# Zero fill of the key and value gradients through a float32 view of the bfloat16 outputs

## The chip, the cores and the metric

The kernel runs on one core of one Trainium2 chip. The metric is the device time of one execution in microseconds; before the change its median is 797.53 us over two runs (797.41 to 797.66). One further execution was taken by the hardware profiler, and all rows below come from that one.

## What is computed

The reference is a decode step with a sliding-window attention and a squared-ReLU layer, and all its gradients. Cut to what matters here:

```python
def _A_ref(x, k_cache, v_cache, wq, wo):        # caches: (2, 8, 32768, 128) bf16
    W = min(4096, max(256, Sk // 4))            # 4096
    k = jnp.repeat(k_cache[:, :, Sk - W:, :], rep, axis=1)
    v = jnp.repeat(v_cache[:, :, Sk - W:, :], rep, axis=1)
    ...
    p = _softmax(scores, axis=-1)
    o = jnp.einsum("bhqk,bhkd->bhqd", p, v)
    return ... @ wo
...
xn = _layernorm(x)
out = x + _A_ref(xn, ...) * _silu(_B_ref(xn, ...))
_out, _vjp = jax.vjp(_f, A_x, A_k_cache, A_v_cache, A_wq, A_wo, B_w1, B_b1, B_w2, B_b2)
```

Only the last 4096 of 32768 cache rows enter the computation. The gradients of both caches have the caches' full shape, so 28672 rows of each of the 2 x 16 (batch, head) regions are zero and have to be written: 2 x 16 x 28672 x 128 elements of two bytes, 234.9 MB. The other outputs together are small beside this.

## The kernel before

**The zero fill.** A tile zt of 128 partitions x 7168 bytes (type uint8, lines 80 and 81) is cleared once by VectorE. The function zf (lines 91 to 103) issues one DMA on GpSimd's queue that writes zeros over a run of rows of one region. Its source is zt, one byte for each element; its destination is the bfloat16 output, so that the DMA casts each zero byte to a two-byte zero as it writes. A partition's share is cut into groups of zg = 56 rows (32 rows in every fourth region, line 117), and the source is repeated over the groups with to_broadcast. One contiguous run of the destination is thus 56 x 128 x 2 = 14336 bytes, or 8192 bytes with 32 rows.

A region's main job (line 134) fills with 128 partitions as far as that goes and then the remainder. Six regions have a job ahead of it (line 127, by the skip plan of line 116) with 120 partitions. The counter zcur (line 102) follows the partition counts of all fills, and zf_tiny (lines 108 to 114) puts in fills of some elements to bring the counter to a wanted value; the plan decides by it where the 120-partition jobs fall. zf_tiny has a slice of its own and doesn't go through zf.

**The order of the work.** Nine fill jobs are issued ahead of everything else (line 159). The others are handed out over the 16 blocks of the main loop (line 448) and what is left after it (line 571). On GpSimd they stand in one instruction stream with the multiplications that make bdq and bddo (line 443).

**The rest.** After a short prologue (layer norm, the squared-ReLU layer forward, transposes of w1 and w2), the main loop runs over 8 heads and 2 batches. For each it loads 1 MB of the v and of the k window on SyncE's queue (lines 368 and 370), one block ahead; transposes them on TensorE; makes scores, softmax and their gradients; and makes dv and dk by matmuls against bddo and bdq, which GpSimd prepares. dv_st and dk_st (1 MB each, bfloat16) are stored from ScalarE's queue (lines 535 and 542), as are the gradients of wo and wq (lines 357 and 569), and the weight slices are loaded on that queue too. An epilogue makes the gradients of w1, w2, the biases and x, and stores them from SyncE's queue (lines 592 to 672). The last of the dw1 stores is on line 649.

Of the kernel before, what the change touches and what calls it, by code (L numbers as in the profile page):

```python
# [12 lines left out]
F32 = mybir.dt.float32  # L13
# [4 lines left out]
def kernel(  # L18
# [27 lines left out]
    _, HKV, SK, DH = A_k_cache.shape  # L46
# [33 lines left out]
    zt = const.tile([P, ZE], mybir.dt.uint8, name="zt")  # L80
# [4 lines left out]
    def _kof(n):  # L85
        for k in range(16, 0, -1):
            if n % k == 0:
                return k
        return 1

    def zf(o, q, r0, nent, rows_per_ent, zg=None):
        zg = zg or ZG
        b, hk = divmod(q, HKV)
        nr = nent * rows_per_ent
        if rows_per_ent % zg == 0:
            v = o[b, hk, r0:r0 + nr, :].rearrange("(r p g) d -> p r (g d)", p=nent, g=zg)
            src = zt[0:nent, 0:zg * DH].unsqueeze(1).to_broadcast([nent, rows_per_ent // zg, zg * DH])
        else:
            v = o[b, hk, r0:r0 + nr, :].rearrange("(p g) d -> p (g d)", p=nent)
            src = zt[0:nent, 0:rows_per_ent * DH]  # L100
        dma_zero.dma_start(out=v, in_=src)  # L101
        zcur[0] = (zcur[0] + _kof(nent)) % 16
        return r0 + nr
# [16 lines left out]
    def region_jobs(qi):  # L120
        o = out_2 if qi < B * HKV else out_3
        q = qi % (B * HKV)
        st = {"r": 0}

        zg = ZG_OF(qi)

        def j_skip():
            eng, nch = skip_plan[qi]
            adv = (eng + 1 - zcur[0]) % 16
            if adv:  # L130
                zf_tiny(adv)
            st["r"] = zf(o, q, st["r"], 120, nch * ZG)

        def j_main():
            rem = ZR - st["r"] - (P if qi == SCRAP_Q else 0)
            n_full = rem // (P * zg)
            if n_full:
                st["r"] = zf(o, q, st["r"], P, n_full * zg, zg)
            rem = ZR - st["r"] - (P if qi == SCRAP_Q else 0)
            if rem:  # L140
                nent = [n for n in (128, 64, 32, 16) if rem % n == 0][0]
                st["r"] = zf(o, q, st["r"], nent, rem // nent)
            if qi == SCRAP_Q:
                st["r"] = zf(o, q, st["r"], P - 1, 1)
                if scrap_pos[0] < DH:
                    zf_tiny(DH - scrap_pos[0])

        return ([j_skip] if qi in skip_plan else []) + [j_main]
# [554 lines left out]
```

## Time and profile before

| what | value |
|---|---|
| median of two runs | 797.53 us |
| span of the profiled execution | 795.6 us |
| busy PE / DVE / ACT / POOL | 402.2 / 265.6 / 210.0 / 315.3 us |
| bytes moved by DMA | 326.85 MB, mean 411 GB/s |
| zero fill: DMAs on line 101 | 42, mean issue 769 ns |
| last store issued (line 649) | 730.3 us |

The span runs from the first to the last instruction of the profiled execution. The median of the runs is 1.9 us above it. The page has the busy time of the engines, the span in 40 slices of 19.9 us, the DMA queues (q0 is GpSimd's, q1 SyncE's, q10 ScalarE's), a chain of waits, the costliest groups of instructions, and the DMA issues with their time to landing. A packet is one descriptor's worth of data, here one contiguous run; its size in the records is that of its destination. Shares of 16 engines can add to a little over 100%, since the records of packets overlap at their ends.

### The profile page before, as it was taken

The numbers are of one execution on the slowest core, as the hardware profiler recorded it, in microseconds if no ns is written. First come the engines' busy times: TensorE is split into PE (matmuls) and PEld (weight loads), VectorE is DVE, ScalarE is ACT, GpSimd is POOL, SyncE is SP. The second block draws the span as 40 slices with busy tenths as digits, with TensorE's granted clock in tenths as the row PEclk, the third lists the DMA queues.
The fourth block names the chain that finished last, engine by engine and source line by source line (L and its number), as shares of the span: only waits on it lengthen the run. The fifth ranks groups of instructions, "written<-read, shape, count | busy, mean of one in ns | idle before, by whom it ended". The sixth has DMA issues, their size and how long they took to land.

```text
span 795.6 us, 11174 instructions
## 1 busy us (share of the span) xinstructions
PE 402.2 (51%) x4776; PEld 277.0 (35%) x4776; DVE 265.6 (33%) x550; ACT 210.0 (26%) x384; POOL 315.3 (40%) x249
## 2 busy tenths in 40 slices
PE   4566444573446546634475358446733686276000
PEld 3466124352424444423272326243522353131000
DVE  3243322361323423611352136223611453754000
ACT  2232310360133314501342135203600450034000
POOL 3001791098109531881080719800826192700000
PEclk9978655895588659955697589656955795555555
DMA  9999999999999999999999999999999999999981
GB/s 361 421 422 424 427 427 423 431 416 417 423 428 424 417 420 428 421 421 421 428 420 422 424 426 423 425 422 430 422 420 422 430 425 420 431 429 425 416 340 57
DMA packets 37794, 326.85 MB, mean 411 GB/s; under 512 B 3008, under 2 KB 3144, under 8 KB 11016
## 3 DMA queue, kind: packets, MB, share of 16 engines
q0 software_dynamic: 20288, 234.89, 71.6%
q10 hardware_dynamic: 11296, 50.34, 16.5%
q1 hardware_dynamic: 6160, 40.91, 13.2%
q8 instruction: 37, 0.61, 0.3%
q14 instruction: 13, 0.11, 0.0%
HBM read 45.62 MB, written 280.50 MB: 410 GB/s over the span
## 4 chain that ended last, share of the span: by engine, by line
DMA 48%; PE 19%; DVE 9%; issue 6%; ACT 5%; POOL 2%; another core or an unknown queue 2%; ACTq 0%; POOLq 0%; DVEq 0%
DMA out_dram<-dv_st 20%; DMA knat<-in_A_k_cache_dram 15%; DMA out_dram<-dwo_st 7%; DMA out_dram<-zt 5%; ACT dv_st L193 3%; DMA out_dram<-dk_st 2%; PE ov L531 2%; PE s_ps L467 2%; PE ok L538 2%; PE tp L463 2%; PE dp_ps L506 2%; PE tp L495 1%; PE dq_ps L524 1%; DVE dk_st L195 1%
## 5 line engine op out<-in xcount | busy, mean ns | idle before, releaser
L443 POOL TENSOR_TENSOR bddo<-dorep,maskbd 128x1024 bf16<-128x1024 bf16 x64 | 133.6, 2114 | 90.5 <-ACT dorep L438 90.5
L443 POOL TENSOR_TENSOR bdq<-qrep,maskbd 128x1024 bf16<-128x1024 bf16 x64 | 133.4, 2110 | 0.0
L101 POOL DMA_DIRECT2D out_dram<-zt x42 | 32.2, 769 | 203.5 <-DMA out_dram<-zt 201.8
L463 PE MATMUL tp<-ident_bf,knat 128*128 128x128 bf16 x512 | 56.6, 280 | 74.8 <-DMA knat<-in_A_k_cache_dram 71.3
L463 PEld LDWEIGHTS <-knat 128*128 128x128 bf16 x512 | 44.7, 127 | 98.8 <-DMA knat<-in_A_k_cache_dram 72.8
L193 ACT CAST dv_st<-ov 128x512 bf16<-128x512 f32 x80 | 44.4, 593 | 125.3 <-PE ov L531 81.2
L531 PE MATMUL ov<-bddo,p_blk 128*128 128x512 bf16 x128 | 51.4, 486 | 50.3 <-ACT dv_st L193 39.6
L195 DVE CAST dv_st<-ov 128x512 bf16<-128x512 f32 x48 | 33.2, 693 | 100.7 <-PE ov L531 57.9
L355 PE MATMUL wps<-ds_rows,o_rows_alt 2*128 2x512 bf16 x32 | 17.4, 600 | 73.0 <-ACT dwo_st L193 73.0
L538 PE MATMUL ok<-bdq,ds_blk 128*128 128x512 bf16 x128 | 46.2, 422 | 15.9 <-DVE dk_st L195 6.0
L195 DVE COPY kT<-tp 128x1024 bf16<-128x1024 bf16 x48 | 32.8, 682 | 58.4 <-PE tp L463 58.4
L193 ACT CAST dk_st<-ok 128x512 bf16<-128x512 f32 x80 | 44.6, 589 | 26.7 <-PE ok L538 22.5
L495 PE MATMUL tp<-ident_bf,vnat 128*128 128x128 bf16 x512 | 42.9, 235 | 7.6 <-DVE vT L195 4.5
L495 PEld LDWEIGHTS <-vnat 128*128 128x128 bf16 x512 | 36.6, 107 | 26.3 <-issue 24.4
L195 DVE CAST dk_st<-ok 128x512 bf16<-128x512 f32 x48 | 32.8, 689 | 28.1 <-PE ok L538 24.8
L195 DVE CAST dwo_st<-wps 128x512 bf16<-128x512 f32 x16 | 11.1, 691 | 85.5 <-DMA out_dram<-dv_st 81.8
L193 ACT CAST dwo_st<-wps 128x512 bf16<-128x512 f32 x16 | 8.7, 588 | 112.0 <-DMA out_dram<-dv_st 111.6
L195 DVE COPY vT<-tp 128x1024 bf16<-128x1024 bf16 x48 | 32.3, 682 | 14.7 <-PE tp L495 14.5
L531 PEld LDWEIGHTS <-p_blk 128*128 128x128 bf16 x128 | 12.7, 119 | 59.6 <-ACT dv_st L193 25.5
L538 PEld LDWEIGHTS <-ds_blk 128*128 128x128 bf16 x128 | 10.3, 103 | 40.2 <-DVE dv_st L195 17.3
L519 PEld LDWEIGHTS <-ds_blk 128*128 128x128 bf16 x16 | 1.7, 104 | 64.2 <-issue 64.2
L195 DVE COPY woT_s<-tp 128x1024 bf16<-128x1024 bf16 x8 | 19.5, 2432 | 10.5 <-PE tp L394 10.5
(240 smaller groups left out, 674.9 us busy)
## 6 DMA issues: line engine op xcount, KB each, us to landing
out_dram<-zt POOLq DMA_DIRECT2D x25, 7168.0 KB, 135.2
out_dram<-zt POOLq DMA_DIRECT2D x4, 6720.0 KB, 146.6
vnat<-in_A_v_cache_dram SPq DMA_DIRECT2D x16, 1024.0 KB, 16.6
knat<-in_A_k_cache_dram SPq DMA_DIRECT2D x16, 1024.0 KB, 20.9
out_dram<-dv_st ACTq DMA_DIRECT2D x16, 1024.0 KB, 22.0
out_dram<-dk_st ACTq DMA_DIRECT2D x16, 1024.0 KB, 17.1
out_dram<-zt POOLq DMA_DIRECT2D x1, 6144.0 KB, 100.5
out_dram<-zt POOLq DMA_DIRECT2D x1, 5120.0 KB, 98.6
```

The source lines that it names most:

```text
L101: dma_zero.dma_start(out=v, in_=src)
L193: nc.scalar.copy(out=out_ap, in_=in_ap)
L195: nc.vector.tensor_copy(out=out_ap, in_=in_ap)
L355: nc.tensor.matmul(wps[:], lhsT=o_rows_alt[:, j, :], rhs=ds_rows[:, :], start=True, stop=True)
L443: nc.gpsimd.tensor_tensor(out=bd[:, c0:c0 + BDC, :], in0=rep[:, :].unsqueeze(1).to_broadcast([P, BDC, DH]), in1=maskbd[:, c0:c0 + BDC, :], ...
L463: nc.tensor.transpose(tp[:, j, :], knat[:, g * 8 + j, :], ident_bf[:, :])
L467: nc.tensor.matmul(s_ps[:], lhsT=zq[:, 31 - c:159 - c], rhs=kT[:, c, :], start=(c == 0), stop=(c == NC_ - 1))
L495: nc.tensor.transpose(tp[:, j, :], vnat[:, g * 8 + j, :], ident_bf[:, :])
L506: nc.tensor.matmul(dp_ps[:], lhsT=zdo[:, 31 - c:159 - c], rhs=vT[:, c, :], start=(c == 0), stop=(c == NC_ - 1))
L524: nc.tensor.matmul(dq_ps[:], lhsT=knat[:, c, :], rhs=dsT[:, c, :], start=(c == 0), stop=(c == NC_ - 1))
L531: nc.tensor.matmul(ov[:], lhsT=p_blk[:, :], rhs=bddo[:, g * 4:(g + 1) * 4, :].rearrange("p c d -> p (c d)"), start=True, stop=True)
L538: nc.tensor.matmul(ok[:], lhsT=ds_blk[:, :], rhs=bdq[:, g * 4:(g + 1) * 4, :].rearrange("p c d -> p (c d)"), start=True, stop=True)
```

## The change

The fill's destination is viewed as float32 in place of bfloat16, so that it has half as many elements of twice the size, and the source slice is halved to match. Each zero byte of the source becomes four zero bytes of the output. The runs of the destination, the number of DMAs, their order and the tile zt are unchanged; half of zt is no longer read. zf_tiny keeps its two-byte destination.

```diff
@@ -93,11 +93,11 @@
         b, hk = divmod(q, HKV)
         nr = nent * rows_per_ent
         if rows_per_ent % zg == 0:
-            v = o[b, hk, r0:r0 + nr, :].rearrange("(r p g) d -> p r (g d)", p=nent, g=zg)
-            src = zt[0:nent, 0:zg * DH].unsqueeze(1).to_broadcast([nent, rows_per_ent // zg, zg * DH])
+            v = o[b, hk, r0:r0 + nr, :].bitcast(F32).rearrange("(r p g) d -> p r (g d)", p=nent, g=zg)
+            src = zt[0:nent, 0:zg * DH // 2].unsqueeze(1).to_broadcast([nent, rows_per_ent // zg, zg * DH // 2])
         else:
-            v = o[b, hk, r0:r0 + nr, :].rearrange("(p g) d -> p (g d)", p=nent)
-            src = zt[0:nent, 0:rows_per_ent * DH]
+            v = o[b, hk, r0:r0 + nr, :].bitcast(F32).rearrange("(p g) d -> p (g d)", p=nent)
+            src = zt[0:nent, 0:rows_per_ent * DH // 2]
         dma_zero.dma_start(out=v, in_=src)
         zcur[0] = (zcur[0] + _kof(nent)) % 16
         return r0 + nr
```

## The prediction

> **What bounds the kernel now.** I read the page's time slices first, since they say whether one resource is full all the time.
>
> ```profile
> DMA  9999999999999999999999999999999999999981
> GB/s 361 421 422 424 427 427 423 431 416 417 423 428 424 417 420 428 421 421 421 428 420 422 424 426 423 425 422 430 422 420 422 430 425 420 431 429 425 416 340 57
> DMA packets 37794, 326.85 MB, mean 411 GB/s; under 512 B 3008, under 2 KB 3144, under 8 KB 11016
> ```
>
> Each digit is a fortieth of the span (19.9 us). The 16 DMA engines are at 9 from the first slice to the 38th and move 416 to 431 GB/s in slices 2 to 38. No compute engine comes near this: the page's first part has PE at 402.2 us of 795.6, the others at 40% or less. So the bound is the DMA engines' throughput on 326.85 MB, and 326.85 MB over the mean of 411 GB/s is 795 us, the span itself.
>
> Next, whose bytes these are: the page's table of DMA queues.
>
> ```profile
> q0 software_dynamic: 20288, 234.89, 71.6%
> q10 hardware_dynamic: 11296, 50.34, 16.5%
> q1 hardware_dynamic: 6160, 40.91, 13.2%
> HBM read 45.62 MB, written 280.50 MB: 410 GB/s over the span
> ```
>
> Columns are packets, MB, and the time of the packets as a share of 16 engines' span. q0 is GpSimd's queue, on which the zero fill alone is issued: 32 regions x 28672 rows x 256 B = 234.88 MB. So the page counts the bytes of the destination, not of the source, which is half as large. One engine on q0 moves 234.89 MB / (0.716 x 16 x 795.6 us = 9114 us) = 25.8 GB/s; on q10, 50.34 / 2100 = 24.0; on q1, 40.91 / 1681 = 24.3. The cast queue is not the slow one.
>
> Third, the end of the span, by the windows view (columns: PE, PEld, DVE, ACT, POOL busy us, PE clock, DMA share, GB/s).
>
> ```profile
> 720.00:740.00 20.00, 9.36 (x23) 2.59 (x21) 7.02 (x12) 6.84 (x12) 0.00 (x0) 0.50 1.03 423
> 740.00:760.00 20.00, 0.00 (x0) 0.00 (x0) 0.00 (x0) 0.00 (x0) 0.00 (x0) 0.50 1.03 410
> 760.00:780.00 20.00, 0.00 (x0) 0.00 (x0) 0.00 (x0) 0.00 (x0) 0.00 (x0) 0.50 0.73 291
> 780.00:795.60 15.60, 0.00 (x0) 0.00 (x0) 0.00 (x0) 0.00 (x0) 0.00 (x0) 0.50 0.08 31
> ```
>
> After 740 us no engine computes: the last store, of dw1, is issued at 730.3 us (the view of line 649) and the last 55 us are DMA backlog alone. The engines do not run dry together: share 0.73, then 0.08, about one engine of 16 at the end. Evenly shared, the span would end 0.27 x 20.0 + 0.92 x 15.6 = 19.8 us earlier. The page's chain of waits ends at 730 us and names dv_st and knat transfers; their length is queueing behind this backlog, so I don't read it as a latency bound.
>
> Fourth, the zero fill's own line, in the waits view and in the page's DMA issues.
>
> ```profile
> POOL out_dram L101 <- DMA out_dram<-zt: 201.8, 16, 31.2
> POOL out_dram L112 <- DMA out_dram<-zt: 44.5, 4, 16.6
> out_dram<-zt POOLq DMA_DIRECT2D x25, 7168.0 KB, 135.2
> ```
>
> GpSimd stands 246 us waiting for earlier fills before it can issue the next. The fill is always ahead of its drain, so issue cost (42 x 769 ns = 32 us on line 101) is covered.
>
> **The price of a packet.** The trace keeps each DMA packet's duration and size. Grouped (mean ns; size is that of the destination):
>
> ```
> zero fill 1->2 byte   14336 B x13288  551    8192 B x4992  325
> w1/w2 load, no cast   14336 B x256    559
> k/v load, no cast                            8192 B x4096  326
> dv/dk store, no cast                         8192 B x4096  323
> ```
>
> From the fill's two sizes: (551 - 325) ns / (14336 - 8192) B gives 27.2 GB/s for an engine plus about 24 ns fixed. The pair that decides is the store of dv/dk against the fill at 8192 B: same direction, same destination size, and the store reads 8192 B from SBUF where the fill reads 4096. Doubling the source changes 325 to 323 ns. The time of a packet follows the destination's bytes.
>
> **What the Trainium skill says.** "DMA: Bandwidth & Descriptors", section "Where 436 GB/s comes from", gives 16 ports x 32 B x 850 MHz = 435.2 GB/s, which is 27.2 GB/s an engine: the slope above is that figure, and the slices' 416 to 431 GB/s are 96 to 99% of it. The same section names about 358 GB/s as the HBM limit of a core; the trace's 410 over the whole span contradicts that for one core alone, and the measurement decides. "SWDGE vs HWDGE vs iDMA" says that a cast needs the GpSimd path; both versions have one. "Queues, rings and completion order" says that an engine takes turns between queues at packets; the landing times of loads (knat 20.9 us for 1 MB) agree with sharing. No page that I found prices a cast by its element widths.
>
> **The change part by part.** Each region's fill describes the same HBM bytes as half as many float32 elements; a full row of the fill is 56 x 128 / 2 = 3584 elements from 3584 B of zt, where it was 7168 from 7168.
>
> Destination: 234.88 MB before and after, in the same runs of 14336 or 8192 B, so 13288 + 4992 large descriptors as before. At 551 and 325 ns: change 0.
>
> Source: read traffic from SBUF falls from 117.4 to 58.7 MB. Value taken: 0. The work that hides it is the write side of the same packet: at 27.2 GB/s the read of a large packet is 264 ns now and 132 after, beside a write of 527. If read and write ran one after the other the packet would take at least 791 ns, and it takes 551, so serial reads are excluded. Gain bound: the uncast copy of 14336 B takes 8 ns more with 7168 B more read (other direction, so only a hint); 3584 B less might then save 4 ns: 13288 x 4 / 16 engines = 3.3 us. The 8192 B pair points to -1 ns saved, that is none. If even the cover went, there is nothing to pay, since the read only shrinks.
>
> Cast to four bytes: not seen in the trace. Per destination byte it makes half as many elements, 6.8 per ns and engine at full rate, where 13.6 are sustained now; so the element rate cannot bind if it is one rate for all types. Value taken 0; lower end 0 (the destination's slope is already the ceiling); upper end open, priced as a rival.
>
> Issue: 42 instructions on line 101 and 7 on line 112, the same partition counts, so the cursor of line 102 and the skips of line 132 keep their values. Value 0; covered by 246 us of waiting on GpSimd in any case. Small leftovers (512 of 3584 B at 155 ns, 127 of 256 B at 38 ns and some more) are about 150 us of engine time, 9 us of the span, and keep their destination sizes. The memset of zt (1.55 us) is untouched. No wait is added; zf_tiny on line 112 is not edited.
>
> Sum: 795.6 + 0 = 795.6 us of span; the median of the runs lies 1.9 us above it (797.53), so 797.5 us.
>
> **The rivals.** First, a gain in the fixed part: the lighter read lets an engine start the next packet earlier. All 24 ns gone from 18280 large packets is 18280 x 24 / 16 = 27 us, giving 770; half of it gives 784. It is over 2% (16 us) from 59% of the fixed part on. For it: engines run at 423 GB/s, not 435. Against: halving the source from store to fill already bought nothing.
>
> Second, on the other side: the conversion to a four-byte output runs below the port's rate. Its place is the 13288 + 4992 large packets, its price the excess per packet. 16 us of span are 16 x 16000 / 18280 = 14 ns a packet, 2.5%: from there on the change is slower by 2%. If the output came at half rate, 14336 B would take 527 ns more and 8192 B 301: (13288 x 527 + 4992 x 301) / 16 = 532 us, giving 1330. For it: nothing in the trace covers this cast. Against: the two-byte cast costs nothing measurable beside a copy.
>
> Third, turn-taking: with shorter reads the fill may run further ahead inside an engine and loads land later. Nothing is lost while the queues are full, since a delayed load only lets more fill through; it costs only if the last store moves from 730 towards 770 us, or if the uneven tail of 19.8 us grows. Worth -3 to +6 us: 794 to 804.
>
> Fourth, that the narrower source is not what reaches the engines, for instance that the rows are cut otherwise: with equal descriptors it is again 797.5; twice as many would cost 18280 x 24 ns / 16 = 27 us, giving 825. Nothing in the trace speaks for it.
>
> **How the numbers follow.** No change, 794 to 800: 0.75. A small gain down to 782: 0.07. A gain of over 2%: 0.05. A small loss up to 813, by the tail or turn-taking: 0.06. A loss of over 2%, slow cast or split rows: 0.07. About 2% is what a measurement here can tell from no change. Faster 0.05, same 0.75 + 0.07 + 0.06 = 0.88, slower 0.07. The range of 788 to 803 takes the likeliest case, the nearer half of each small one, and leaves out under 0.2.
>
> **What would show it.** Right: q0 at about 20288 packets, 234.89 MB and 71 to 72%; slices at 416 to 431 GB/s; packets of 14336 B at 551 ns; GpSimd's waits for zt near 246 us. Wrong: a q0 share over 73% with longer packets (slow cast); a packet count that doubles (split rows); packets under 540 ns or slices near 435 GB/s (a gain in the fixed part); unchanged packets with a longer last slice (the tail).

## The result, and the profile after

The changed kernel takes 807.58 us (807.22 to 807.93), the kernel before 797.53: ratio 1.0126, 95% interval 1.0096 to 1.0155. It is slower by 1.3%, where no change was forecast. A further measurement gave 807.89 us, ratio 1.0130 (1.0112 to 1.0148).

The profiled execution has a span of 805.4 us, 9.8 longer than before. First its time slices, which answer to the lines shown of before.

```profile
DMA  9999999999999999999999999999986999989996
GB/s 367 420 422 427 430 423 427 429 421 416 423 429 432 415 423 421 427 430 422 423 421 429 413 375 424 423 431 414 429 330 247 364 391 421 431 351 427 421 396 268
DMA packets 37794, 326.85 MB, mean 406 GB/s; under 512 B 3008, under 2 KB 3144, under 8 KB 11016
```

Packets and bytes are the same to the last digit, and so is the rate in most slices. What is new is a hole: slices 30 to 33 (584 to 664 us) move 247 to 391 GB/s; slices 24 and 36 are down too, at 375 and 351. In return the end, where the kernel before fell from 340 to 57, is fuller at 396 and 268.

Next the DMA queues.

```profile
q0 software_dynamic: 20288, 234.89, 72.6%
q10 hardware_dynamic: 11296, 50.34, 22.7%
q1 hardware_dynamic: 6160, 40.91, 17.8%
```

The fill (q0) barely moved, from 71.6 to 72.6%. The copies did: ScalarE's queue went from 16.5 to 22.7% and SyncE's from 13.2 to 17.8% with unchanged packets. The packet records say where: each copy ends in up to 16 packets of 4 bytes, read here as those that announce its completion. They last 808 ns in the mean, against 43 before (1568 of them on the two queues), while a copy's data packets of 8192 B went from 325 to 342 ns only.

The waits view (us in total, times, longest us) has another order. Two lines of the kernel before:

```profile
POOL bddo L443 <- ACT dorep L438: 90.5, 10, 20.0
PE tp L463 <- DMA knat<-in_A_k_cache_dram: 71.3, 9, 16.1
```

And of the kernel after:

```profile
POOL bddo L443 <- ACT dorep L438: 240.0, 14, 35.0
PE tp L463 <- DMA knat<-in_A_k_cache_dram: 115.2, 12, 19.7
POOL out_dram L101 <- DMA out_dram<-zt: 61.0, 3, 31.9
```

Before, GpSimd waited 201.8 us on line 101 for fills ahead of it: the fill always had work waiting. Now it waits 61.0 there and 240.0, instead of 90.5, for the blocks' own work (dorep), ahead of which it cannot issue more fill. PE waits 115.2 us for k, where it waited 71.3. The stores of dk show how far the blocks have fallen back, in the view of line 542; the first of these lines is of the kernel before.

```profile
L542 ACTq DMA_DIRECT2D out_dram<-dk_st x16: 338/338/354, 106.3 to 713.1; - x16
```

The second is of the kernel after.

```profile
L542 ACTq DMA_DIRECT2D out_dram<-dk_st x16: 338/338/358, 105.9 to 783.6; - x16
```

The first block ends as early as before, the sixteenth 70.5 us later. The way there is uneven: by the starts of the 16 dk stores the lateness is 19.8 us at the fourth block, 47.7 at the seventh and 82.1 at the eleventh, and then it shrinks a little. The last dw1 store is issued at 800.3 us instead of 730.3, and the span ends 5.1 us after it.

```profile
L649 SPq DMA_DIRECT2D out_dram<-dw_st_7325 x1: 332/332/332, 800.3 to 800.3; - x1
```

So the end is now set by the blocks and the epilogue, no more by a backlog of fill.

The bytes give a balance, by the windows view. It says when the rate was lower and when higher, not yet why. The kernel before:

```profile
560.00:720.00 160.00, 89.32 (x1047) 56.66 (x1047) 69.98 (x131) 43.68 (x83) 72.88 (x53) 0.65 1.05 425
720.00:795.60 75.60, 9.36 (x23) 2.59 (x21) 7.02 (x12) 6.84 (x12) 0.00 (x0) 0.50 0.76 304
```

The kernel after:

```profile
560.00:720.00 160.00, 88.86 (x1055) 60.55 (x1055) 51.82 (x113) 43.16 (x86) 75.01 (x58) 0.67 1.03 376
720.00:805.40 85.40, 48.29 (x426) 24.21 (x423) 37.62 (x70) 23.84 (x44) 22.41 (x17) 0.60 1.07 370
```

At the steady 424 GB/s, the hole costs 160 x (1 - 376 / 424) = 18.1 us, and 360 x 3 / 424 = 2.5 us are lost from 200 to 560 us (421 GB/s). The end gives back 75.6 x (1 - 304 / 424) = 21.4 less 85.4 x (1 - 370 / 424) = 10.9, that is 10.5 us. Together +10.1 us, for a span longer by 9.8.

### The profile page after: what moved, and what is told of

It reads as the page before. It is cut to its first block, busy times and chain, and to the rows that moved or that the text cites. A ratio compares the mean times of both kernels' runs of the same rounds, so it can differ in the third digit from the quotient of the medians.

```text
span 805.4 us, 11174 instructions
## 1 busy us (share of the span) xinstructions
PE 416.9 (52%) x4776; PEld 286.9 (36%) x4776; DVE 258.8 (32%) x550; ACT 210.2 (26%) x384; POOL 314.9 (39%) x249
## 3 DMA queue, kind: packets, MB, share of 16 engines
q0 software_dynamic: 20288, 234.89, 72.6%
q10 hardware_dynamic: 11296, 50.34, 22.7%
q1 hardware_dynamic: 6160, 40.91, 17.8%
## 4 chain that ended last, share of the span: by engine, by line
DMA 63%; PE 17%; DVE 6%; issue 5%; ACT 4%; POOL 2%; another core or an unknown queue 2%; ACTq 0%; POOLq 0%; DVEq 0%
DMA knat<-in_A_k_cache_dram 20%; DMA out_dram<-dv_st 18%; DMA out_dram<-dk_st 13%; DMA out_dram<-dwo_st 8%; DMA out_dram<-zt 5%; PE ov L531 2%; PE ok L538 2%; PE tp L463 2%; PE s_ps L467 2%; ACT dv_st L193 2%; PE dq_ps L524 1%; PE dp_ps L506 1%; PE tp L495 1%; POOL bddo L443 1%
## 5 line engine op out<-in xcount | busy, mean ns | idle before, releaser
L463 PE MATMUL tp<-ident_bf,knat 128*128 128x128 bf16 x512 | 56.6, 279 | 118.3 <-DMA knat<-in_A_k_cache_dram 115.2
L538 PE MATMUL ok<-bdq,ds_blk 128*128 128x512 bf16 x128 | 51.1, 465 | 36.2 <-ACT dk_st L193 26.7
L193 ACT CAST dk_st<-ok 128x512 bf16<-128x512 f32 x80 | 44.5, 589 | 57.4 <-PE ok L538 28.6
L495 PEld LDWEIGHTS <-vnat 128*128 128x128 bf16 x512 | 39.4, 113 | 32.9 <-issue 31.3
L495 PE MATMUL tp<-ident_bf,vnat 128*128 128x128 bf16 x512 | 45.3, 245 | 6.6 <-DVE vT L195 3.4
```

Of the source, the lines that this page charges most:

```text
L193: nc.scalar.copy(out=out_ap, in_=in_ap)
L463: nc.tensor.transpose(tp[:, j, :], knat[:, g * 8 + j, :], ident_bf[:, :])
L495: nc.tensor.transpose(tp[:, j, :], vnat[:, g * 8 + j, :], ident_bf[:, :])
L538: nc.tensor.matmul(ok[:], lhsT=ds_blk[:, :], rhs=bdq[:, g * 4:(g + 1) * 4, :].rearrange("p c d -> p (c d)"), start=True, stop=True)
```

## Experiments

Where an expectation gives the time of a dry fill, it is on the clock of the packet records, which starts about 10 us ahead of the span: its 602 to 656 us are 592 to 646 us of the span.

**The fill alone: does the wider cast cost anything?** Everything but the fill is left out, with the narrow and the wide cast.

```diff
-    zf_issue(ZF_FIRST)
-    ... (all that follows)
+    zf_issue(len(zf_jobs))
+    attn.close()
```

> Only the zero fill is left (cast one byte to two, all 49 DMAs issued at once); attention, epilogue and all other outputs are left out. 234.9 MB over 16 engines at 27.2 GB/s and 24 ns a packet (551 and 325 ns) is (13288 x 551 + 4992 x 325) / 16 = 559 us, less where packets overlap: span 545 to 570 us. Both theories expect the same here; it is the yardstick for the next run.

> The same fill alone, cast one byte to four. Overtaking theory (the four-byte fill costs the same per byte, but with half the source it runs further ahead inside the engines and the copies beside it complete later): within 0.5% of the fill with one to two, packets of 14336 B again at about 551 ns, since there is no copy to overtake. Slow-cast theory (the rise of the mean packet from 551 to 564 ns in the profile after is a cost of the cast): packets at 564 ns and a span 2.3% longer, some 13 us.

Measured: 559.2 us with one byte to two, 559.1 with one to four. The slow-cast rival falls. The records of the large packets did grow, from 554 to 575 ns, but with the same total: records overlap, and the DMA share of q0 reads 102.8% in one and 107.5% in the other.

```profile
q0 software_dynamic: 20288, 234.89, 102.8%
q0 software_dynamic: 20288, 234.89, 107.5%
```

So longer records don't make a slower fill, and the 564 ns of these packets in the kernel after are no sign of a slow cast.

**A probe for the copies.** All fills, and beside them 16 rounds of a 1 MB load, a copy on VectorE and a 1 MB store; nothing else is computed. Each probe is one execution.

```diff
+    zf_issue(len(zf_jobs))
+    for n in range(16):
+        nat = wsl1.tile([P, NC_, DH], BF16, tag="knat")            # one buffer
+        dma_load.dma_start(out=nat[:], in_=A_k_cache[...])
+        st = rowp.tile([P, NC_, DH], BF16, tag="dk_st")            # one buffer
+        nc.vector.tensor_copy(out=st[:], in_=nat[:])
+        dma_store.dma_start(out=out_2[...], in_=st[:])
```

> A probe: all zero fills, cast one byte to two, and beside them 16 times a 1 MB load of k, a copy on VectorE and a 1 MB store of it into the rows of dk, with one buffer each; nothing else is computed, all other outputs are left out. The landing of loads and stores is here free of the attention's feedback. Theory: loads and stores land in 15 to 25 us; completion packets of 4 B on the copy queues at about 40 ns.

> The same probe with the fill cast one byte to four. Theory (copies complete later beside the four-byte fill): median landing of loads or stores longer by 2 us or more, the last store later by 30 us or more, completion packets at several hundred ns, while the whole span, set by the bytes, stays within 1%. Rival (copies are late in the change only because of what the blocks do): landings within 1 us of the probe with one to two.

The page's DMA issues (KB each, median us from issue to landing) for the probe with one to two:

```profile
nat<-in_A_k_cache_dram SPq DMA_DIRECT2D x16, 1024.0 KB, 16.2
out_dram<-st ACTq DMA_DIRECT2D x16, 1024.0 KB, 16.4
```

And with one to four:

```profile
nat<-in_A_k_cache_dram SPq DMA_DIRECT2D x16, 1024.0 KB, 24.5
out_dram<-st ACTq DMA_DIRECT2D x16, 1024.0 KB, 26.9
```

The last store is issued at 411.6 us instead of 275.8, while the span stays (634.9 us with one to two, 634.2 with one to four): the copies come later and the sum of the bytes takes as long as before.

The packet records of the 16 loads divide a landing into three parts (medians, us).

| part of a 1 MB load | one to two | one to four | one to four, half runs |
|---|---|---|---|
| from issue to the first data packet | 5.8 | 11.2 | 10.7 |
| from the first to the end of the last of 128 data packets | 8.8 | 8.6 | 7.0 |
| from there to the end of the last completion packet | 0.9 | 4.3 | 4.1 |

So the data move as fast as before, but they start 5.4 us later, and their completion is announced 3.4 us later in the median. The completion packets of loads and stores (512) last 27 ns in the median and at most with the narrow cast. With the wide cast the median is 1129 ns, the commonest value 7464 ns (150 of them), and the longest 14346. The last column is of the next run.

**Is the late completion a number of fill packets, or of bytes?** The wide probe with runs of half the length (ZG 56 to 28, and 32 to 16 in every fourth region).

> The probe (all fills, and 16 times load, copy, store) with the four-byte cast and runs of half the length. If an engine's lead is a number of fill packets (about 14 of 14336 B in 7.5 us), the slow completion packets take half as long, about 3.7 us; if it is bytes, 7.5 us as with the long runs. Landings lie between the two other probes (16 and 25 us for loads) in either case, since turns by packet let the copies' data through earlier.

```profile
nat<-in_A_k_cache_dram SPq DMA_DIRECT2D x16, 1024.0 KB, 22.4
```

Loads land in 22.4 us, and the commonest value of the completion packets is 3774 ns. At 27.2 GB/s 7464 ns are 14.2 packets of 14336 B (527 ns each), and 3774 ns are 14.3 of 7168 B (264 ns each): the commonest wait of a completion is a number of fill packets, about 14. The wait ahead of the first data is not: it stays at 10.7 us where it was 11.2.

**Short runs in the full kernel.**

```diff
-    ZG_OF = lambda qi: (ZG if qi % 4 != 3 else 32)
+    ZG_OF = lambda qi: (ZG if qi % 4 != 3 else 16)
-    ZG = 56
+    ZG = 28
```

The jobs with 120 partitions, whose rows are counted in ZG, become half as long with this.

> The kernel before with runs of half the length (28 and 16 rows: 7168 and 4096 B of destination, 3584 and 2048 B of source), cast one to two. If the engines' read-ahead is a matter of source bytes, copies are delayed as much as before: last dk store near 713 us, and the time rises only by the fixed part of the added packets, 18280 x 24 ns / 16 = 27 us at most, less where packets overlap: 798 to 825 us. If turns go by packet, the fill gets half as much per turn, copies go faster than before and the last dk store comes at 680 us or earlier.

> The change with runs of half the length (7168 and 4096 B of destination, 1792 and 1024 B of source), cast one to four. Overtaking by the ratio of source to destination: copies delayed as in the change, last dk store 50 us or more later than in the same kernel with one to two, and completion packets of 4 B on the copy queues at several hundred ns in the mean. Turns by packet: as the kernel with one to two and short runs, within 10 us for the last dk store. Slow cast: last dk store as with one to two, longer fill packets (over 2%).

Measured: 797.05 us (ratio 0.9995, 0.9986 to 1.0003) with one to two, 796.82 us (0.9991, 0.9983 to 1.0000) with one to four: no loss at all with the wide cast. Yet its blocks are late by 45.8 us against the narrow cast. Line 542, one to two and then one to four:

```profile
L542 ACTq DMA_DIRECT2D out_dram<-dk_st x16: 338/338/359, 114.1 to 715.0; - x16
```

```profile
L542 ACTq DMA_DIRECT2D out_dram<-dk_st x16: 338/338/358, 114.2 to 760.8; - x16
```

So lateness by itself costs nothing up to here. The expected "50 us or more" was somewhat high. The completion packets last 1549 ns in the mean, longer than in the change with its 808, though its last block ends 22.8 us earlier (760.8 us against 783.6): the mean of these records is a sign of the delay and no measure of it. And "680 us or earlier" for turns by packet did not come: with one to two, k lands in 16.2 us instead of 20.9, but the last dk store stays at 715.0. The 19424 more packets cost nothing, where up to 27 us had been allowed.

**A wait taken from the blocks.** In the change dwo_st shares dv_st's single buffer; here it has its own, in the room that the unused half of zt leaves.

```diff
-    ZE = ZG * DH
+    ZE = ZG * DH // 2
-        dwo_st = stage.tile([P, REP, D], BF16, tag="dv_st")
+        dwo_st = stage.tile([P, REP, D], BF16, tag="dwo_st")
```

> The change, with a staging buffer of its own for dwo_st (it shared dv_st's single buffer), room for it taken from the half of zt that is no longer read. Theory (copies complete later beside the four-byte fill, the blocks' chain of waits stretches, the fill runs dry at 602 to 656 us and the chain's end is bare at 783): the eight waits of dwo_st for dv_st's store (109 us on ScalarE in the change) go, the last dk store comes at 750 us or earlier, the fill does not run dry for over 5 us, and the time is 795 to 800 us. Rival (the loss is DMA throughput lost to the cast or to contention): 805 to 810 us whatever the waits.

> The change with a staging buffer of its own for dwo_st, profiled once more. Theory: in an execution of 798 to 800 us the fill is not dry for over 5 us at a time ahead of its end, and the last dk store comes earlier than the change's 783 us; in one of 808 us it is dry for 20 us as in the profile of that group. Rival (removing the wait does nothing to the supply of the fill): dry for 20 us or more with 798 us too.

Measured: 798.81 us, ratio 1.0024 (1.0010 to 1.0038); 18 of 20 executions lie from 798.1 to 800.3, two at 808.7 and 810.5. One of these two was profiled, so a second profile was taken, of an execution of 798.7 us. There the last dk store comes at 774.1 us, later than the 750 expected but 9.5 earlier than in the change, and the time is 8.9 us shorter. But what I had expected of the fill is wrong: it is dry for 17 and for 11 us, where it was for 25 and 11 in the change, and 560 to 720 us moves 378 GB/s, as little as there (376).

```profile
560.00:720.00 160.00, 87.21 (x1069) 58.40 (x1069) 53.61 (x115) 46.98 (x91) 76.12 (x57) 0.68 1.06 378
720.00:797.00 77.00, 43.43 (x403) 22.64 (x401) 38.31 (x64) 18.20 (x34) 19.09 (x12) 0.54 1.16 393
```

The time came back at the end (393 GB/s instead of 370). The dry stretch is thus a sign that the blocks are late; what goes with the time is when the blocks end. The rival of throughput lost to the cast falls too, since the cast is the same.

**Half of the change.** The wide view only for the regions of one gradient: first the key gradient's (issued first), then the value gradient's.

```diff
+        wide = o is out_2          # the other kernel: o is out_3
+        ob = o[b, hk, r0:r0 + nr, :].bitcast(F32) if wide else o[b, hk, r0:r0 + nr, :]
+        w = DH // 2 if wide else DH
```

> Only the fills of the key gradient's regions (the first half of the jobs) cast one byte to four; the second half casts one to two. Theory: lateness gathers only in the first half, the last dk store comes near the middle of 713 and 783, about 745 us, with the fill still there to cover it, so nearly nothing is lost: 796 to 800 us. Rival (a loss in proportion to the bytes cast to four): half of 10 us, 801.5 to 803.5 us.

> The reverse: only the fills of the value gradient's regions (the second half of the jobs) cast one byte to four. Theory: last dk store again near 745 us, no dry stretch of over 5 us, 796 to 800 us. Rival (in proportion): 801.5 to 803.5 us.

Measured: 797.19 us (0.9993, 0.9986 to 1.0000) for the first half: nothing lost, last dk store at 755.5 us. For the second half 801.20 us (1.0026, 1.0010 to 1.0041), in two groups: 7 of 20 at 796.1 to 796.5, 13 at 800.8 to 803.6. The profile is of the upper group, with the last dk store at 778.1 us instead of the 745 expected. Its fill is dry for no more than 6.6 us, and yet time is lost. Line 545 is here the line of the dk stores, for the first half and then for the second:

```profile
L545 ACTq DMA_DIRECT2D out_dram<-dk_st x16: 338/338/357, 106.0 to 755.5; - x16
```

```profile
L545 ACTq DMA_DIRECT2D out_dram<-dk_st x16: 338/338/360, 106.1 to 778.1; - x16
```

A loss in proportion to the bytes, equal for both halves, is ruled out. Why the executions of the second half form two groups is open.

The two profiles also show where the lateness gathers. Half of the fill's bytes have gone at 379 us with the first half wide and at 399 with the second. The table has the starts of the dk stores, by block, in us after those of the kernel before.

| wide view for | 1 | 4 | 7 | 8 | 11 | 13 | 16 |
|---|---|---|---|---|---|---|---|
| all fills (the change) | -0.4 | 19.8 | 47.7 | 54.6 | 82.1 | 72.2 | 70.5 |
| the first half | -0.3 | 20.9 | 44.5 | 44.5 | 42.2 | 42.6 | 42.4 |
| the second half | -0.2 | 1.1 | 3.3 | 12.8 | 48.4 | 64.8 | 65.0 |

The seventh block's dk store is at 381 us in the one and at 340 us in the other. Lateness is added while wide fill is moving, and hardly any is added or recovered while narrow fill is. The completion packets switch with it: their mean is 951 ns up to 400 us and 70 ns after it with the first half wide, 53 and 1125 ns with the second. Within one program, blocks of the same work are thus delayed or not with the width of the fill beside them. The two halves together make more lateness (42.4 and 65.0 us) than the whole change (70.5), whose blocks stop losing ground at the eleventh, while its fill is running dry.

**The change once more.**

> The changed kernel itself once more, in several rounds beside the kernel before, since the kernels with part of the change lay in two groups some 5 us apart. Theory (the loss is the bandwidth that goes unused while the fill is dry): 805 to 809 us, or two groups, with the profile's dry stretches over 10 us in sum where the time is over 800 us. Rival (a constant cost): one group at 807.5 us.

Measured: 807.4 to 808.5 us in four executions, one group, with the fill again dry for 26 and 11 us. Theory and rival both allowed one group, so this confirms the size and tells them not apart.

**No cast at all, short runs.** zt is bfloat16, with ZG 28 and 16 as above, in the full kernel and with the fill alone (one execution).

```diff
-    zt = const.tile([P, ZE], mybir.dt.uint8, name="zt")
+    zt = const.tile([P, ZE], BF16, name="zt")
```

> Short runs (7168 and 4096 B) without any cast: zt is bfloat16, the source as wide as the destination. With one to two and one to four in the same runs it makes a ladder of the source's width. If the copies' delay grows with the lightness of the source, copies complete as early as with one to two or earlier: last dk store at 715 us or before, completion packets at 40 ns; time 795 to 799 us, set by the bytes.

> Only the zero fill, in short runs (7168 and 4096 B) and without a cast; everything else is left out. The full kernel with this fill took 848.9 us where the two casts took 797. If the uncast read as wide as the write costs throughput by itself, the fill alone takes 585 us or more instead of 559 (the ratio of the two full kernels' bytes per us, 385 to 411); if it costs only beside the copies, or only by how the 120-partition jobs are spread over the engines, 555 to 575 us with whole slices at 425 GB/s and a longer tail.

Measured: 848.9 us (ratio 1.0625, 1.0571 to 1.0678), far off the 795 to 799 expected, and 634.3 us for the fill alone against 559 with casts. Completion packets last 9 ns in the mean, the shortest of all, so that side of the expectation held, though the last dk store came at 765.1 us rather than by 715. The slices of the fill alone:

```profile
GB/s 287 415 413 356 255 416 416 415 409 368 276 410 414 408 406 375 276 380 412 407 414 386 320 402 409 413 415 384 276 339 417 413 386 380 402 415 416 411 279 64
```

Its best slices are at 402 to 417 GB/s, and about every sixth dips to 255 to 339; with casts and long runs the slices are at 402 to 439 without such dips. The length of the runs alone is not the cause: the probe with short casting runs moved 422 GB/s. The dips have a place in the program. The lowest slices begin at 63, 158, 253, 348 and 443 us, and counted by bytes the first five of the six 120-partition jobs begin at 58, 156, 253, 350 and 444 us. The casting fill alone passes these jobs without a dip. Why the uncast one doesn't, and how much of the loss is the wider read, stays open: a fill without a cast in long runs, or without these jobs, wasn't tried.

## Why the prediction was wrong

**The bound and the price of packets: right.** The fill is limited by the bytes of its destination, the cast to four bytes is free, descriptors and bytes did not change, the memset, the issues and the small leftovers neither (the two fills alone, 559.2 and 559.1 us). The forecast's sum of zero is right for all that it summed.

**"The time of a packet follows the destination's bytes": shown for the two casts only.** Between them it held. The uncast fill, with a wider source, took 634.3 us for the same destination bytes, so the stores of dv and dk, a small share of the bytes, were too narrow a ground for a rule about every width. Whether the width is the cause there is open, as said above.

**The chain of waits: the failed step.** The prediction set it aside: it ends at 730 us, and "I don't read it as a latency bound". That gave the last 55 us of fill backlog no price as slack. The runs give one. Last dk store and span: 713.1 and 795.6 (before), 755.5 and 795.5 (first half), 760.8 and 795.3 (short runs), then 774.1 and 796.9 (own buffer), 778.1 and 800.0 (second half), 783.6 and 805.4 (the change), 784.1 and 806.1 (the change once more). While the store is early the span stays at 795; beyond, it is the last dk store plus 22 us, in which the epilogue's stores are issued and land. The two lines meet at about 773 us. So the kernel before had some 60 us of slack (an estimate from these profiles), and the change used 70.5. One point is off: the profile of the own buffer at 779.4 us has a span of 806.9, where the rule gives 801. In that profile the fill still runs at 789 us, while in the change it has ended at 782, and the 1 MB of dwq_st, issued at 780.8 us, lands at 804.5 instead of some 5 us after its issue. So there the last stores wait beside fill once more; why the fill is later in that execution is open.

**Turn-taking, the third rival: the mechanism in kind, mis-sized.** The prediction said that the fill may run further ahead inside an engine and loads land later, that "nothing is lost while the queues are full", and that it costs once the last store moves "from 730 towards 770 us". The later landings and the cost at the end were seen: the last store moved to 800.3. That the fill runs ahead inside an engine was not seen itself. The point from which it costs was set somewhat early; 773 us for the last dk store is about 790 for the last store. But the worth of -3 to +6 us, and the chance of 0.06 for a loss of this size by the tail or turn-taking, rested on no estimate of the shift. The term is 70.5 us of lateness at the last block, less 60 of slack, some 10 us, and the time rose by 10.05 (the slack is read from the same runs, so this is a check of consistency and no forecast). What it lacked was that a block waits for several transfers in a row, each of which can land some 8 us later (16.2 and 24.5 us for a load of the probe). "A delayed load only lets more fill through" was true, but that fill is taken from the stock that hides the end.

**The completion.** The section "Queues, rings and completion order" of the Trainium skill's "DMA: Bandwidth & Descriptors" says that the increment of a semaphore lands only after every earlier write of that engine, across its queues. The probe agrees in this: a load's data take 9 us in both, and beside the wide cast a completion packet most often lasts 7464 ns, the time of about 14 fill packets. The prediction drew turn-taking alone from that section. But the wait of the completion is the smaller part of the delay, 3.4 us in the median; 5.4 us more pass before a load's first data packet (medians of the parts, which don't quite add to the 8.3 us of the whole). Why a transfer waits for so much fill at both ends with the wide cast, and for little with the narrow one, was not isolated. That the engine reads the fill ahead while it writes, since a read of 3584 B is a quarter of the write's bytes where it was half, is only argued.

**What would show it.** Unchanged packet counts and bytes were listed as signs of being right, and they came; so was a steady rate in the slices, which did not (247 GB/s in the hole). The signals that spoke were the share of q1 and q10 and the 4-byte packets, which the list doesn't name, and GpSimd's wait for zt, expected near 246 us and found at 77 (61.0 on line 101).

## What to carry to other kernels

In a kernel that keeps the DMA engines full, background traffic that costs the same per byte can still delay the start and the completion of every other transfer. So price the waits that stand in a row, and the slack until their chain sets the end, before calling a change of the background free. Measure that slack (here 60 us between the last block's store and the point where it shows) as carefully as the bound itself. Here half the run length of the fill brought the last block's store from 783.6 to 760.8 us, inside the slack, and the loss was gone, at no cost in throughput. In the probe it took the commonest wait of a completion from 7.5 to 3.8 us and left the wait ahead of the data; which of the shorter landings saved the blocks' time was not taken apart. No version here beat the kernel before clear of the measurement.

## What the runs showed of the hardware

- The duration of a packet in the records isn't its cost: 554 and 575 ns for the same packet count in the same 557 us of span; the records then add to 102.8 and 107.5% of the engines.
- Beside a fill that casts one byte to four, a 1 MB load lands in 24.5 us in the median, beside one that casts one to two in 16.2, though both fills take 559 us alone. The first data packet comes 11.2 us after the issue instead of 5.8, and the last completion packet ends 4.3 us after the data instead of 0.9.
- The delay follows the fill that is moving at the time: with the wide cast in one half only, completion packets last 951 and 70 ns in the mean before and after 400 us, or 53 and 1125 ns.
- Halving the runs of a casting fill from 14336 to 7168 B (19424 more packets) changed the full kernel by -0.36 us, within the measurement; 24 ns of fixed cost in each packet's record would have been up to 27 us.
- A fill without a cast, in runs of half the length, moved 371 GB/s, where the casting ones moved 422 in long runs. Casting fill in short runs, beside copies, moved 422 too.
